# Attention and mixture-of-depths on one core: the gate taken from the gathered rows, a shorter index, and a redrawn order of work

## The chip, the cores and the metric

The kernel runs on one core of a Trainium2 chip. The metric is the device time of one execution in microseconds. The kernel before takes 217.61 us, the median of three runs (217.41 to 217.83).

## The reference

The inputs are q, k and v of 8 batches, 12 heads, 448 tokens and 64 features, a gate vector of 768, and two weight matrices. All arrays are fp32.

```python
scores = scale * np.matmul(q, k.transpose(0, 1, 3, 2))       # scale = 1/8
attn = np.maximum(scores, 0.0) ** 2 / S                      # S = 448
x = np.matmul(attn, v)                                       # heads side by side: [8, 448, 768]
# then, for each batch b
s = x @ w_gate                                               # one score a token
top_idx = the 128 tokens with the highest s
xe = x[top_idx]
ye = np.maximum(xe @ w1, 0.0) @ w2                           # 768 -> 1024 -> 768
out = x;  out[top_idx] = x[top_idx] + sigmoid(s[top_idx])[:, None] * ye
```

## The kernel before

One program does everything, and the order of its work is written out by hand: `ORDER` is a string of some 1,350 items such as `S,6,2,1`. The loop at the end reads them one by one and calls the function of that name, so each engine's queue holds its instructions in the order of the string. Engines run in order, each waits on semaphores where a tile isn't ready, and a waiting instruction holds up all that is behind it on its engine.

**Attention.** A batch has six pairs of heads, numbered t = 6b to 6b + 5, and two pairs make a unit u (u = 0, 2, 4 are batch 0, u = 6, 8, 10 are batch 1, and so on to u = 46). `T,u` transposes q and k of a unit on TensorE (112 small matmuls) into two PSUM banks; `TE,t,engine` copies one pair's result to SBUF on ScalarE (A) or VectorE (D). For the first unit q and k are apart: `Tq`, `Tk`, `TEq`, `TEk`. `S,u,i,banks` makes the scores of 64 keys, i = 0 to 6, in one of two pairs of banks. `R,u,i` (L242) is their relu on ScalarE into SBUF. `Q,u,g` (L249) squares a group of two or three of them on VectorE. `V,u,i` multiplies with v and sums over i in two banks; `X,t,engine` copies the result, transposed x, to SBUF. Only ScalarE does R, only VectorE does Q.

**Experts.** For batch b: `g` (six matmuls with the gate vector repeated over 128 columns) gives the scores as rows, `bc` copies them to SBUF, `col` and `colE` turn them into columns. `XR` and `XRE` transpose x back to rows (for the last batches the DMA transpose `XB` does it, and `XP`, `XPE` for the last two pairs). `rk` counts for each token how many score higher, `less` (six 1-column matmuls) adds the counts across blocks, and `hot` makes a one-hot matrix of the chosen tokens. `xe` gathers the chosen rows with that matrix, already transposed, `xeE` copies them out. `h` and `hE` are the first expert layer (eight blocks in two halves), `y` and `yE` the second, with the gate as the scale of `yE`. `ST` writes the batch's plain rows to the output and `ADD` adds the gated rows with an indirect DMA. The last batch does without the addition: `xs` gathers its chosen rows, `yX` adds them, and `PUT` writes them.

**The gate and the index before.** `tok` holds for each token its number, in two parts, and its score in three bf16 parts, made by the four VectorE operations of `p` (L362, L364, L366, L368). `sel` multiplies the one-hot matrix with these five columns. `sE` then copies the result (L408), adds the two parts of the number into `idx` (L410) and the three parts of the score into `g_` (L412), and `sig` (L416) takes the sigmoid on ScalarE. `tok` has four copies, for batches in flight together.

**Loads.** All but the first q, the gate vector and the DMA transposes are issued by GpSimd (POOL). `L,b,i,r` loads half r (six heads) of q, k or v (i = 0, 1, 2) of batch b and casts it to bf16; `W,0` and `W,1` load w1 and w2. From batch 3 on a load also waits for a given R, so that the loads are spread (`PACE`). `Zp` builds constants on GpSimd and stands among the loads. The gate vector `wgf` is loaded by SyncE inside `C,0`, after a memset on VectorE, and `Zw` spreads it on VectorE.

**Zero matmuls.** `D,n,cols,bank` issues n matmuls of zeros that nobody reads.

A tile in PSUM takes one of eight banks by its tag, and a bank is used again when its last reader is done. The matmuls of all the helpers but `col` have line L179.

## Time and profile before

| | us |
|---|---|
| median of three runs | 217.61 |
| the profiled execution, its time | 217.12 |
| its span, first to last instruction | 215.4 |
| TensorE matmuls busy | 196.4 (91%) |
| ScalarE busy | 181.7 (84%) |
| VectorE busy | 174.8 (81%) |
| GpSimd busy | 71.6 (33%) |
| 168 score evictions R on ScalarE | 144.1 |
| 72 squarings Q on VectorE | 88.8 |

The mean granted clock of TensorE is 0.989. Busy shares are averages over a start, a long stretch in which attention of one batch and experts of another run side by side, and a last stretch that has experts alone; what counts is the engine that the others wait for in each of them. A TensorE that is called busy may be waiting, since the ends of matmuls are modelled.

### The profile page before, as it was taken

The page shows a single profiled execution, that of the slowest core. Times are in us where ns is not written, and L with a number is a line of the kernel's source. Part 1 is how long each engine was busy: PE and PEld are TensorE (multiplying, and loading weights), DVE is VectorE, ACT ScalarE, POOL GpSimd, SP SyncE. Part 2 cuts the span into 40 slices and gives each one's busy share as a digit, 9 for nine tenths or more (in the row PEclk, how much of TensorE's full clock was granted, in tenths as well). Part 3 has the DMA queues.
Part 4 walks back from the last instruction along what each step waited for, and adds up shares of the span by engine and source line. Part 5 has one row for each costly group of instructions (what it writes and reads, how often), then busy time and mean ns, then how long its engine had stood idle before and what let it go on. Part 6 is the DMA issues. An engine that isn't in the chain of part 4 may idle for free. (4 is left out here: it accounts for less than half of the span.)

```text
span 215.4 us, 8419 instructions
## 1 busy us (share of the span) xinstructions
PE 196.4 (91%) x3745; PEld 118.4 (55%) x3745; DVE 174.8 (81%) x355; ACT 181.7 (84%) x252; POOL 71.6 (33%) x103
## 2 busy tenths in 40 slices
...
GB/s 118 171 174 201 207 213 206 206 209 271 270 206 306 237 166 6 251 233 110 130 87 330 177 134 64 148 309 135 65 142 210 83 50 163 148 98 159 137 64 73
DMA packets 32532, 35.90 MB, mean 167 GB/s; under 512 B 7728, under 2 KB 29872, under 8 KB 31600
## 3 DMA queue, kind: packets, MB, share of 16 engines
...
q10 hardware_dynamic: 144, 0.23, 0.4%
q14 instruction: 7, 0.06, 0.1%
...
## 5 line engine op out<-in xcount | busy, mean ns | idle before, releaser
L242 ACT ACTIVATE r_sb<-s_ps 128x896 bf16<-128x896 f32 x168 | 144.1, 940 | 5.1 <-PE s_ps L179 4.9
L249 DVE TENSOR_TENSOR a_sb<-r_sb 128x1792 bf16<-128x1792 bf16 (+1 forms) x72 | 88.8, 1247 | 4.2 <-ACT r_sb L242 3.9
L179 PE MATMUL s_ps<-qkt 64*64 64x448 bf16 x672 | 62.9, 372 | 4.3 <-ACT r_sb L242 2.8
L179 PE MATMUL o_ps<-a_sb,v_sb 64*64 64x448 bf16 x672 | 46.2, 360 | 2.2 <-DVE a_sb L249 2.1
L179 PEld LDWEIGHTS <-qkt 64*64 64x64 bf16 x672 | 24.4, 105 | 29.6 <-issue 17.9
L268 DVE COPY qkt<-t_ps 128x896 bf16<-128x896 bf16 (+1 forms) x38 | 22.1, 604 | 8.8 <-PE t_ps L179 8.8
L179 PE MATMUL ye_ps<-w_sb,hT 128*128 128x384 bf16 x128 | 27.9, 329 | 0.4 <-ACT hT L264 0.4
L179 PEld LDWEIGHTS <-v_sb 64*64 64x64 bf16 x672 | 20.5, 107 | 13.4 <-issue 7.5
L179 PE MATMUL h_ps<-xeT,w_sb 128*128 128x128 bf16 x384 | 27.9, 220 | 0.0
L179 PEld LDWEIGHTS <-w_sb 128*128 128x128 bf16 x384 | 22.1, 98 | 7.8 <-issue 7.2
L82 POOL DMA_DIRECT2D q_sb<-in_q_dram x18 | 11.9, 667 | 39.5 <-ACT r_sb L242 38.2
L270 DVE TENSOR_SCALAR xT_sb<-o_ps 128x448 bf16<-128x448 f32 x28 | 17.1, 621 | 7.1 <-PE o_ps L179 6.9
L82 POOL DMA_DIRECT2D k_sb<-in_k_dram x20 | 14.5, 732 | 21.1 <-ACT r_sb L242 17.4
L82 POOL DMA_DIRECT2D v_sb<-in_v_dram x18 | 11.9, 672 | 27.0 <-ACT r_sb L242 17.9
L489 POOL DMA_INDIRECT out_dram<-gye,idx x7 | 13.8, 1966 | 10.9 <-ACT xeT L264 5.7
L179 PEld LDWEIGHTS <-hT 128*128 128x128 bf16 x128 | 10.6, 97 | 10.9 <-issue 6.3
L374 DVE SCALAR_TENSOR_TENSOR trash<-bc_sb,cols,tie 64x64 bf16<-64x64 f32 (+3 forms) x32 | 14.5, 477 | 0.7
L179 PE MATMUL xe_ps<-hot_sb,x_sb 128*128 128x128 bf16 x192 | 14.4, 219 | 0.1
L179 PE MATMUL sc_ps<-xT_sb,wg_rep 128*128 128x448 bf16 x48 | 13.7, 354 | 0.6 <-DVE xT_sb L270 0.5
L264 ACT ACTIVATE xT_sb<-o_ps 128x448 bf16<-128x448 f32 x20 | 11.3, 572 | 3.4 <-PE o_ps L179 3.4
L264 ACT ACTIVATE qkt<-t_ps 128x896 bf16<-128x896 bf16 (+1 forms) x12 | 10.3, 864 | 4.1 <-PE t_ps L179 4.0
L179 PEld LDWEIGHTS <-x_sb 128*128 128x128 bf16 x192 | 11.3, 97 | 4.2 <-issue 3.4
...
## 6 DMA issues: line engine op xcount, KB each, us to landing
...
```

The source lines that it names most:

```text
L82: return [nc.gpsimd.dma_start(out=t_sb[b % NBUF][HALF[r], h0:h1], in_=heads(src, b, r, h0, h1)) for r in halves]
L179: nc.tensor.matmul(out=out_, lhsT=lhsT, rhs=rhs, start=start, stop=stop, skip_group_check=True, **kw)
L242: relus[u, i] = nc.scalar.activation(out=r_sb[u, g][:, i - GROUP.index(g)], in_=s_ps.pop((u, i))[:, :, :S], func=AF.Relu).ins
L249: nc.vector.tensor_tensor(out=a_sb[u, g], in0=r, in1=r, op=ALU.mult)
L264: nc.scalar.activation(out=out_, in_=in_, func=func or AF.Copy, scale=scale)
L268: nc.vector.tensor_copy(out=out_, in_=in_)
L270: nc.vector.tensor_scalar(out=out_, in0=in_, scalar1=scale, scalar2=None, op0=ALU.mult)
L374: nc.vector.scalar_tensor_tensor(out=self.more[p, c, 128 * c:], in0=self.bc_[p, 128 * c:S], scalar=self.cols[p, c:c + 1], in1=tie[p, :S - ...
L489: nc.gpsimd.indirect_dma_start(out=out[0:self.b + 1].rearrange("b s d -> (b s) d"), out_offset=bass.IndirectOffsetOnAxis(ap=self.idx[:, :1 ...
```

## The change

- **Gate.** For all batches but the last, the score of a chosen row is computed again from the gathered row: ahead of the first `y` of half 0, six 1-column matmuls multiply the gathered rows with one column of the repeated gate vector, into a 385th column of y's bank, and `sig` reads that column from PSUM. `p` is left out for these batches, and `tok` has one copy. The last batch keeps the old way.
- **Index.** `sE,0` adds the two parts of the number straight from PSUM into `idx`. For all but the last batch `sel` has two columns and `sE,0` is the only one of the three operations.
- **Order.** The whole string is redrawn. Among other things: `C,0` is now on VectorE and `C,1` on ScalarE; `TEq` stands ahead of `Tk`; the loads of batches 1 and 2 and of the weights come in another order (q and k of batch 2 ahead of w1), and `Zp` stands among the last of them; `T,6` and `T,10` come ahead of the `V` of unit 4, `T,18` ahead of the scores of unit 16; `XP` of the last two pairs comes behind the last two `g`. Counting the letters, ScalarE has 5 fewer TE, 3 fewer X and 1 fewer yE, and 3 more XRE, 3 more hE and 2 more xeE; VectorE has the reverse.
- **Zero matmuls.** 55 in place of 33: eleven in place of eight of 512 columns at the start, and 44 in place of 25 of 128 columns, the later ones up to the scores of unit 6.

```diff
--- before.py
+++ after.py
@@ -123,8 +123,7 @@
     slot_row = const.tile([128, NC, CAP], mybir.dt.float16)
     tie = const.tile([128, S], BF16)
     chosen = const.tile([CAP, HD], FP32)
-    NTK = 4
-    tok = const.tile([128, NTK, NC, 5], BF16)
+    tok = const.tile([128, NC, 5], BF16)
 
     def Zp():
 
@@ -133,7 +132,7 @@
 
         for r in range(2):
             for i in range(2):
-                nc.gpsimd.iota(tok[HALF[r], :, :, i], pattern=[[0, NTK], [i, NC]], base=4 * i * r,
+                nc.gpsimd.iota(tok[HALF[r], :, i], pattern=[[i, NC]], base=4 * i * r,
                                channel_multiplier=4 - i, allow_small_or_imprecise_dtypes=True)
 
 
@@ -326,13 +325,13 @@
         def __init__(self, b):
             self.b = b
             self.xT = xT_sb[b % NX]
-            self.tk = tok[:, b % NTK]
+            self.last = b == B - 1
             self.bc_ = bc_sb[b % 2]
             self.hot_ = hot_sb[b % 2]
             self.more = trash_[b % 2]
             for pool, name, shape, dt in (
                     (tiny, "cols", [128, NC], FP32), (tiny, "rem", [128, NC], FP32),
-                    (tiny, "rank_", [128, NC], FP32), (tiny, "sel_", [CAP, 5], FP32),
+                    (tiny, "rank_", [128, NC], FP32), (tiny, "sel_", [CAP, 3], FP32),
                     (tiny, "idx", [CAP, 1], INT32), (tiny, "g_", [CAP, 1], FP32)):
                 setattr(self, name, pool.tile(shape, dt, name=name))
             self.ps = {}
@@ -357,7 +356,8 @@
             nc.vector.tensor_copy(out=self.cols, in_=self.ps["col"])
 
         def p(self, i):
-            tk, cols, rem = self.tk, self.cols, self.rem
+
+            tk, cols, rem = tok, self.cols, self.rem
             if i == 0:
                 nc.vector.tensor_copy(out=tk[:, :, 2], in_=cols)
             elif i == 1:
@@ -398,22 +398,25 @@
                                         op1=ALU.is_equal)
 
         def sel(self, at):
-            self.ps["sel"] = bank(at, [CAP, 5], FP32, "sel_ps")
+            n = 5 if self.last else 2
+            self.ps["sel"] = bank(at, [CAP, n], FP32, "sel_ps")
             for c in range(NC):
-                mm(self.ps["sel"], self.hot_[:, c, :], self.tk[:, c, :], c == 0, c == NC - 1)
+                mm(self.ps["sel"], self.hot_[:, c, :], tok[:, c, :n], c == 0, c == NC - 1)
 
         def sE(self, i):
             sel = self.sel_
             if i == 0:
-                nc.vector.tensor_copy(out=sel, in_=self.ps["sel"])
+                nc.vector.tensor_scalar(out=self.idx, in0=self.ps["sel"][:, 0:1],
+                                        scalar1=self.ps["sel"][:, 1:2], scalar2=None, op0=ALU.add)
             elif i == 1:
-                nc.vector.tensor_tensor(out=self.idx, in0=sel[:, 0:1], in1=sel[:, 1:2], op=ALU.add)
+                nc.vector.tensor_copy(out=sel, in_=self.ps["sel"][:, 2:5])
             else:
-                nc.vector.scalar_tensor_tensor(out=self.g_, in0=sel[:, 4:5], scalar=sel[:, 3:4],
-                                               in1=sel[:, 2:3], op0=ALU.add, op1=ALU.add)
+                nc.vector.scalar_tensor_tensor(out=self.g_, in0=sel[:, 2:3], scalar=sel[:, 1:2],
+                                               in1=sel[:, 0:1], op0=ALU.add, op1=ALU.add)
 
         def sig(self):
-            nc.scalar.activation(out=self.g_, in_=self.g_, func=AF.Sigmoid)
+            nc.scalar.activation(out=self.g_, in_=self.g_ if self.last else self.ps["y", 0][:, 384:385],
+                                 func=AF.Sigmoid)
 
         def xe(self, half, mi, at=None):
             if mi == 0:
@@ -460,7 +463,7 @@
 
         def yX(self, half):
             cols = slice(half * 384, half * 384 + 384)
-            nc.vector.scalar_tensor_tensor(out=self.gye[:, cols], in0=self.ps["y", half],
+            nc.vector.scalar_tensor_tensor(out=self.gye[:, cols], in0=self.ps["y", half][:, :384],
                                            scalar=self.g_[:, 0:1], in1=chosen[:, cols],
                                            op0=ALU.mult, op1=ALU.add)
 
@@ -477,12 +480,17 @@
             if f == 0:
                 if not hasattr(self, "gye"):
                     self.gye = gye_pool.tile([CAP, HD], FP32, name="gye")
-                self.ps["y", half] = bank(at, [CAP, 384], FP32, "ye_ps")
-            mm(self.ps["y", half], self.hT[:, f, :], w2_sb[:, f, half * 384:half * 384 + 384],
+                self.ps["y", half] = bank(at, [CAP, 385], FP32, "ye_ps")
+                if half == 0 and not self.last:
+
+                    for m in range(NM):
+                        mm(self.ps["y", half][:, 384:385], self.xeT[:, m, :], wg_rep[:, m, 0:1],
+                           m == 0, m == NM - 1)
+            mm(self.ps["y", half][:, :384], self.hT[:, f, :], w2_sb[:, f, half * 384:half * 384 + 384],
                f == 0, f == NF - 1)
 
         def yE(self, half, eng):
-            put(eng, self.gye[:, half * 384:half * 384 + 384], self.ps["y", half],
+            put(eng, self.gye[:, half * 384:half * 384 + 384], self.ps["y", half][:, :384],
                 scale=self.g_[:, 0:1])
 
         def ADD(self):
@@ -493,106 +501,104 @@
                 compute_op=ALU.add)
 
     ORDER = """
-    D,8,512,4 C,0,A C,1,D Tq,0,7,6 Tk,0 TEq,0,A TEq,1,D TEk,1,D TEk,0,A D,7,128,4 S,0,1,1 S,0,0,0 R,0,1 R,0,0
-    D,6,128,4 S,0,6,1 T,2,7,6 R,0,6 S,0,2,0 TE,2,D Zw,D R,0,2 D,3,128,4 S,0,4,1 L,1,1,0 TE,3,D R,0,4 D,3,128,4
-    S,0,3,0 Q,0,0 L,1,0,1 R,0,3 D,3,128,4 S,0,5,1 L,1,0,0 R,0,5 D,3,128,4 S,2,4,0 L,1,1,1 Q,0,1 V,0,0,7,6 V,0,1
-    V,0,2 Zp S,2,2,1 T,4,5,4 Q,0,2 R,2,2 V,0,3 V,0,4 R,2,4 TE,5,D S,2,0,1 V,0,5 V,0,6 TE,4,D L,1,2,0 R,2,0
-    S,2,1,0 X,1,D L,1,2,1 R,2,1 X,0,D S,2,5,1 W,0 R,2,5 g,0,0,7 Q,2,0 g,0,1 S,2,3,0 L,2,0,1 S,2,6,1 R,2,3
-    L,2,1,0 V,2,0,6,5 R,2,6 Q,2,1 L,2,0,0 V,2,1 V,2,2 S,4,2,0 L,2,1,1 S,4,4,1 R,4,2 Q,2,2 V,2,3 V,2,4 W,1 R,4,4
-    S,4,3,0 V,2,5 L,2,2,1 V,2,6 R,4,3 S,4,1,1 X,2,D L,2,2,0 R,4,1 X,3,D S,4,0,0 g,0,2 Q,4,1 g,0,3 R,4,0 S,4,5,1
-    R,4,5 S,4,6,0 Q,4,0 R,4,6 V,4,0,6,5 Q,4,2 V,4,1 V,4,2 V,4,3 V,4,4 V,4,5 V,4,6 X,4,A X,5,D T,6,6,4 XR,0,0,5
...
-    h,1,0,1 R,16,5 h,1,0,2 Q,16,1 V,16,0,5,4 V,16,1 V,16,2 L,4,2,1 h,1,1,2 Q,16,2 h,1,1,3 V,16,3 hE,1,1,A V,16,4
-    V,16,5 V,16,6 g,2,0,6 X,16,D X,17,A g,2,1 g,2,2 g,2,3 T,18,5,4 g,2,4 TE,18,A TE,19,D h,1,0,3 g,2,5 hE,1,0,D
...
-    V,46,5 V,46,6 h,6,0,0,7 X,46,D X,47,A h,6,0,1 SC,44 XP,47,5 XP,46,6 XPE,47,A g,7,4 g,7,5 XPE,46,D h,6,0,2
-    bc,7,A SC,47 sel,6,6 h,6,0,3 sE,6,0 col,7,5 sE,6,2 sE,6,1 hE,6,0,A colE,7 rk,7,2 SC,46 sig,6 y,6,1,0,7
...
+    D,11,512,4 C,0,D C,1,A Tq,0,7,6 TEq,0,A TEq,1,D D,7,128,4 Tk,0 TEk,0,A TEk,1,D D,5,128,4 S,0,1,1 S,0,0,0
+    R,0,1 R,0,0 D,6,128,4 S,0,2,1 Zw,D T,2,7,6 R,0,2 S,0,5,0 TE,3,D R,0,5 L,1,1,1 D,3,128,4 S,0,3,1 Q,0,0
+    L,1,1,0 R,0,3 D,3,128,4 S,0,4,0 L,1,0,0 R,0,4 TE,2,D D,3,128,4 S,0,6,1 V,0,0,6,5 L,1,0,1 V,0,1 V,0,2 R,0,6
+    Q,0,1 S,2,2,0 L,2,0,0 T,4,7,4 R,2,2 S,2,3,1 L,1,2,0 Q,0,2 V,0,3 V,0,4 R,2,3 L,2,0,1 S,2,1,0 TE,4,D V,0,5
+    L,1,2,1 R,2,1 S,2,0,1 TE,5,D V,0,6 L,2,1,1 R,2,0 X,0,D S,2,5,0 L,2,1,0 X,1,D D,2,128,4 g,0,0,7 R,2,5 S,2,4,1
+    Q,2,0 W,0 g,0,1 R,2,4 S,2,6,0 W,1 R,2,6 D,3,128,4 S,4,0,1 Q,2,1 V,2,0,6,5 V,2,1 L,2,2,1 V,2,2 R,4,0 S,4,3,0
+    Q,2,2 V,2,3 Zp V,2,4 R,4,3 S,4,4,1 D,2,128,4 V,2,5 R,4,4 V,2,6 S,4,1,0 X,2,D R,4,1 L,2,2,0 D,2,128,4 S,4,2,1
+    Q,4,1 g,0,2 R,4,2 D,2,128,4 S,4,5,0 X,3,D R,4,5 D,2,128,4 T,6,6,4 Q,4,0 g,0,3 TE,6,A S,4,6,1 R,4,6 TE,7,D
+    D,4,128,5 T,10,6,5 S,6,0,0 TE,10,D TE,11,A S,6,1,1 Q,4,2 V,4,0,6,4 R,6,1 V,4,1 V,4,2 V,4,3 V,4,4 R,6,0 V,4,5
+    V,4,6 S,6,2,1 X,4,D R,6,2 S,6,4,0 X,5,D T,8,6,5 R,6,4 L,3,0,0 S,6,5,1 Q,6,0 XR,0,2,4 g,0,4 R,6,5 g,0,5
+    S,6,3,0 bc,0,A TE,9,D L,3,0,1 S,6,6,1 R,6,3 TE,8,D XR,0,0,7 XR,0,1,5 XRE,0,2,D R,6,6 XR,0,3,6 Q,6,1 col,0,4
+    S,8,1,0 XRE,0,0,A S,8,5,1 colE,0 Q,6,2 XRE,0,3,A V,6,0,7,4 V,6,1 V,6,2 R,8,1 V,6,3 V,6,4 rk,0,0 V,6,5 V,6,6
+    R,8,5 S,8,0,0 rk,0,1 rk,0,2 R,8,0 L,3,1,1 S,8,2,1 hot,0,0 rk,0,3 less,0,6 R,8,2 X,6,D S,8,3,0 hot,0,1
+    hot,0,2 R,8,3 g,1,0,7 L,3,1,0 hot,0,3 S,8,4,1 XRE,0,1,D sel,0,6 R,8,4 Q,8,0 ST,0 xe,0,1,0,5 xe,0,1,1
+    xe,0,1,2 X,7,A S,10,1,0 S,8,6,1 xeE,0,1,A g,1,1 sE,0,0 Q,8,1 R,8,6 xe,0,0,0,4 xe,0,0,1 xe,0,0,2 R,10,1
+    V,8,0,6,5 Q,8,2 S,10,0,1 V,8,1 V,8,2 V,8,3 R,10,0 S,10,2,0 V,8,4 xeE,0,0,D V,8,5 V,8,6 R,10,2 S,10,3,1 X,8,D
+    h,0,0,0,4 h,0,0,1 X,9,A L,3,2,0 Q,10,0 h,0,0,2 R,10,3 h,0,0,3 S,10,6,0 hE,0,0,A T,12,6,5 R,10,6 S,10,4,1
...
+    xe,1,1,2 T,18,6,5 xeE,1,1,D S,16,1,1 X,13,A Q,14,2 S,14,4,0 sel,1,7 R,14,4 h,1,1,0,4 h,1,1,1 sE,1,0 TE,18,D
...
+    y,1,1,0,7 y,1,1,1 y,1,1,2 y,1,1,3 colE,2 sig,1 y,1,1,4 XRE,2,2,A rk,2,1 S,20,0,0 XR,2,3,4 rk,2,0 R,20,0
+    y,1,0,2 y,1,0,3 y,1,0,4 y,1,0,5 XRE,2,3,D R,20,2 y,1,0,6 y,1,0,7 hot,2,0 S,18,5,0 ST,2 rk,2,3 T,22,6,4
...
+    y,2,0,5 R,24,6 bc,3,D XR,3,1,7 S,26,1,0 XRE,3,1,D sig,2 col,3,6 R,26,1 y,2,1,0,4 y,2,0,6 colE,3 y,2,0,7
+    rk,3,0 S,24,5,1 yE,2,0,A V,24,0,7,6 V,24,1 rk,3,3 S,26,2,0 R,24,5 rk,3,1 XR,3,0,5 y,2,1,1 y,2,1,2 R,26,2
...
+    XRE,4,3,D XR,4,1,6 colE,4 L,7,0,1 hE,3,1,A rk,4,0 y,3,0,0,7 XRE,4,1,A y,3,0,1 rk,4,1 S,30,6,1 T,32,5,4 sig,3
+    R,30,6 hot,4,0 S,30,3,0 rk,4,3 XR,4,2,6 TE,33,D R,30,3 y,3,0,2 y,3,0,3 TE,32,D y,3,0,4 y,3,0,5 y,3,0,6
...
+    y,4,0,0,5 XRE,5,2,D R,36,6 XR,5,3,7 colE,5 rk,5,1 S,36,3,0 sig,4 XRE,5,3,A T,38,6,4 rk,5,0 S,36,5,1 R,36,3
+    y,4,0,1 TE,38,D y,4,0,2 y,4,0,3 y,4,1,0,7 y,4,0,4 TE,39,D R,36,5 y,4,0,5 y,4,0,6 y,4,0,7 Q,36,1 XR,5,0,6
...
+    S,42,5,1 XB,41 Q,42,0 S,44,2,0 bc,6,A y,5,1,0,6 y,5,0,0,5 R,42,5 y,5,0,1 y,5,0,2 col,6,7 sig,5 Q,42,2
+    y,5,0,3 R,44,2 S,44,0,1 y,5,0,4 y,5,0,5 R,44,0 y,5,1,1 colE,6 S,44,3,0 rk,6,0 V,42,0,7,4 V,42,1 R,44,3
...
+    hE,6,0,A V,46,4 V,46,5 V,46,6 h,6,1,0,6 X,46,A X,47,D h,6,1,1 g,7,4 g,7,5 y,6,0,0,5 bc,7,A XP,47,4 sig,6
+    col,7,7 XPE,47,D SC,44 h,6,1,2 colE,7 h,6,1,3 rk,7,0 y,6,1,0,7 y,6,1,1 hE,6,1,A y,6,1,2 y,6,1,3 rk,7,2 SC,47
+    XP,46,4 y,6,1,4 rk,7,1 y,6,1,5 XPE,46,A y,6,1,6 y,6,1,7 y,6,0,1 hot,7,0 less,7,6 p,7,0 yE,6,1,A rk,7,3 SC,46
...
```

155 lines of the change are left out of this document (67 added, 88 removed).

## The prediction

> **What bounds the kernel now.** I read the busy shares of the page, then the table of stretches, cut at the first score eviction R of batch 0 (9.76 us), the first of batch 1 (33.22) and the end of the last one (192.70). Columns after the stretch: its length, busy time (count) of PE, PEld, DVE, ACT, POOL, then clock, DMA share, GB/s.
>
> ```profile
> PE 196.4 (91%) x3745; PEld 118.4 (55%) x3745; DVE 174.8 (81%) x355; ACT 181.7 (84%) x252; POOL 71.6 (33%) x103
> ...
> L242 ACT ACTIVATE r_sb<-s_ps 128x896 bf16<-128x896 f32 x168 | 144.1, 940 | 5.1 <-PE s_ps L179 4.9
> ```
>
> ```profile
> 0.00:9.76 9.76, 6.31 (x79) 2.84 (x79) 2.29 (x15) 3.04 (x5) 8.12 (x18) 1.00 0.85 138
> 9.76:33.22 23.46, 18.49 (x376) 9.78 (x372) 18.47 (x22) 19.36 (x25) 13.23 (x22) 1.00 1.20 199
> 33.22:192.70 159.48, 155.96 (x3115) 94.53 (x3112) 144.85 (x289) 153.56 (x212) 42.56 (x54) 0.99 0.88 171
> 192.70:215.40 22.70, 15.60 (x184) 11.27 (x182) 9.18 (x31) 5.74 (x12) 7.72 (x10) 0.97 0.79 113
> ```
>
> From the first R to the last, ScalarE (ACT) is the thread that everything hangs on: 168 R take 144.1 us, 0.86 each, and no other engine does them. In the long stretch ACT idles 159.48 - 153.56 = 5.92 us, TensorE (PE) 3.52, VectorE (DVE) 14.63. So the time there is ACT's work plus its stalls, with PE close behind. In the head, 9.76 to 33.22, ACT idles 23.46 - 19.36 = 4.10 us. The last 22.70 us are one chain through the last batch's experts.
>
> The sum is made against the profiled execution: span 215.4, time 217.12, so 1.72 us lie around the span. The median of the runs is 217.61, 0.49 above it; I add that at the end.
>
> **The head: first R.** The chain of the start is in ACT's timeline.
>
> ```profile
> 8.09 0.98 ACT L264 ACTIVATE qkt<-t_ps 128x448 bf16<-128x448 bf16 x2 [2.09 <-PE t_ps L179]
> 9.76 0.92 ACT L242 ACTIVATE r_sb<-s_ps 128x896 bf16<-128x896 f32 x1 [0.69 <-PE s_ps L179]
> ```
>
> TEq and TEk run back to back after both transposes, 0.98 us. The new order puts TEq ahead of Tk, so that it fills the wait for k, and only TEk is left behind the transposes: half of 0.98, so **-0.5**. Bounds: 0, if k's landing is late anyhow, and -0.75, if the three more 512-column zero matmuls bring full clock before the first scores. The other added zero matmuls (33 before, 55 now) stand where PE waits for R or a landing; they cost nothing as long as ACT is behind, else each as much as a short PE slice.
>
> C,0 moves to DVE, and with it the gate vector's load: its memset now follows the cast of q.
>
> ```profile
> wgf<-in_moe_w_gate_dram SPq DMA_DIRECT2D x1, 3.0 KB, 5.4
> ```
>
> It was issued early on SP's otherwise empty queue; now it starts near 5.9 us, after the cast. With the same 5.4 to landing it comes at 11.3, and Zw, TE,3 and the first square Q wait behind it on DVE. PE's first V and S,2 wait for those. I leave 0.8 us of ACT idle in the head for this (bounds 0 and 2.5).
>
> **The head: batch 1's first transposes.** ACT's timeline, then PE's, then POOL's issue of loads:
>
> ```profile
> 30.39 0.55 ACT L264 ACTIVATE xT_sb<-o_ps 128x448 bf16<-128x448 f32 x1 [1.79 <-PE o_ps L179]
> 31.71 0.92 ACT L264 ACTIVATE qkt<-t_ps 128x896 bf16<-128x896 bf16 x1 [0.78 <-PE t_ps L179]
> 33.22 0.92 ACT L242 ACTIVATE r_sb<-s_ps 128x896 bf16<-128x896 f32 x1 [0.15 <-PE s_ps L179]
> ```
>
> ```profile
> 28.62 1.73 PE L179 MATMUL o_ps<-a_sb,v_sb 64*64 64x448 bf16 x28 [1.21 <-DVE a_sb L249]
> 30.98 0.41 PE L179 MATMUL t_ps<-ident,q_sb 64*64 64x64 bf16 x28 [0.64 <-ACT xT_sb L264]
> ```
>
> ```profile
> 20.54 0.66 POOL L82 DMA_DIRECT2D q_sb<-in_q_dram  x1 [0.94 <-DMA q_sb<-in_q_dram]
> 22.22 0.66 POOL L82 DMA_DIRECT2D k_sb<-in_k_dram  x1 [1.03 <-DMA q_sb<-in_q_dram]
> 23.93 0.89 POOL L168 DMA_DIRECT2D w_sb<-in_moe_w_dram  x1 [1.05 <-DMA k_sb<-in_k_dram]
> ```
>
> POOL's waits end on landings, one load about every 1.7 us. The last of batch 1's q and k is in by 23.93, yet T,6 stands behind all of V,4 and starts at 30.98, waiting for an eviction and not for data. The new order sets T,6 and T,10 before V,4, after 20 of the 21 R of batch 0. The first four loads of batch 1 stay first (k, k, q, q), so the data is there. Of the head's 4.10 us idle all but the 0.8 goes: **-3.3**. Bounds: 0, if DVE's squares are late (its 18.47 busy us in the head must then fit before TE,7), and -4.1.
>
> What is late next: W1 now queues behind four more loads (q and k of batch 2).
>
> ```profile
> L166 POOL DMA_DIRECT2D w_sb<-in_moe_w_dram x1: 876/876/876, 17.4 to 17.4; - x1
> ...
> DMA to landing us min/median/max: 18.3/18.3/18.3
> ```
>
> It landed at 35.7; four times 1.7 makes 42.5. Its first reader h,0,0 stands behind R,10,2: batch 1's first R near 29, 17 R at 0.86, some four evictions of about 0.6, less one R that PE runs ahead, so near 45. It is hidden with 2.5 us to spare. W2 has the same loads ahead as before.
>
> **ACT against DVE.** Counting the letters in both orders, ACT loses five TE and three X and one yE and gains three XRE, three hE and two xeE.
>
> ```profile
> L264 ACT ACTIVATE xT_sb<-o_ps 128x448 bf16<-128x448 f32 x20 | 11.3, 572 | 3.4 <-PE o_ps L179 3.4
> ...
> L264 ACT ACTIVATE qkt<-t_ps 128x896 bf16<-128x896 bf16 x10 | 9.3, 929 | 2.0 <-PE t_ps L179 1.9
> ...
> L264 ACT ACTIVATE x_sb<-x_ps 128x768 bf16<-128x768 bf16 x7 | 5.7, 820 | 0.1
> ...
> L264 ACT ACTIVATE hT<-h_ps 128x512 bf16<-128x512 f32 x6 | 3.6, 605 | 3.4 <-PE h_ps L179 3.4
> ...
> L264 ACT ACTIVATE xeT<-xe_ps 128x384 bf16<-128x384 f32 x6 | 3.0, 526 | 0.0
> ...
> L264 ACT ACTIVATE gye<-ye_ps,g__514 128x384 f32<-128x384 f32 x2 | 1.2, 616 | 0.0
> ```
>
> 5 x 0.929 + 3 x 0.572 + 0.616 - 3 x 0.820 - 3 x 0.605 - 2 x 0.526 = 1.65; neighbours overlap by about 0.1 (R: 940 ns long, 858 apart), so **-1.5**, on the path. Bounds -1.7 and 0, the latter where PE sets the pace.
>
> DVE drops the three-way split of the scores in seven batches and two of the three operations on sel.
>
> ```profile
> L362 DVE CAST tok<-cols 128x4 bf16<-128x4 f32 x8 | 1.5, 182 | 0.0
> ...
> L366 DVE CAST tok<-rem 128x4 bf16<-128x4 f32 x8 | 1.4, 169 | 0.0
> L368 DVE TENSOR_TENSOR tok<-rem,tok 128x4 bf16<-128x4 f32 x8 | 1.3, 164 | 0.0
> ...
> L364 DVE TENSOR_TENSOR rem<-cols,tok 128x4 f32<-128x4 f32 x8 | 1.3, 158 | 0.0
> ...
> L408 DVE COPY sel__4942<-sel_ps 128x5 f32<-128x5 f32 x1 | 0.2, 166 | 0.8 <-PE sel_ps L179 0.8
> ```
>
> Seven times 0.673 is 4.7 us less, and two small operations in seven batches another 2.3 at 0.166. What DVE takes over from ACT and gives back nearly cancels. I cost all of it at 0: DVE has 14.63 idle us in the stretch. Bounds -1 (squares earlier) and 0.
>
> **The gate from the rows.** Six 1-column matmuls in seven batches, 42 in all, each with a 128x128 weight load, like those of less:
>
> ```profile
> 38.60 0.41 PE L179 MATMUL less_ps<-ones,trash 128*128 128x1 bf16 x6
> ```
>
> 42 x 0.41 / 6 = 2.9 us on PE, an upper end since the 0.41 has a matmul's own latency once. PE has 3.52 idle us in the stretch, so a part shows: **+0.7**, near the lower end because ACT and not PE holds the path; ends 0 and +2.9. [...] The sigmoid now reads y's bank, so the matmuls of y's half 0 that follow it in the order wait for ACT. That is a new wait; its rival is below.
>
> **Stalls of the long stretch.** ACT's timeline:
>
> ```profile
> 77.39 0.60 ACT L264 ACTIVATE hT<-h_ps 128x512 bf16<-128x512 f32 x1 [1.19 <-PE h_ps L179]
> ...
> 79.72 0.92 ACT L264 ACTIVATE qkt<-t_ps 128x896 bf16<-128x896 bf16 x1 [0.87 <-PE t_ps L179]
> ```
>
> ```profile
> 40.63 4.16 ACT L242 ACTIVATE r_sb<-s_ps 128x896 bf16<-128x896 f32 x5 [0.78 <-PE s_ps L179]
> ```
>
> The pair around 78 us (2.06) is the head's fault again: T,18 comes after V,16, with no scores left to evict. The new order has T,18 ahead of S,16,1. I take -1.5, since PE's h, V and g of that place must still be done somewhere. The 0.78 stands in a stretch of half clock:
>
> ```profile
> 39.86:43.27 3.41, 3.26 (x34) 1.57 (x37) 2.96 (x8) 2.64 (x4) 1.24 (x2) 0.50 1.18 211
> 36.44:39.85 3.41, 1.87 (x20) 0.85 (x20) 3.20 (x9) 3.41 (x5) 1.21 (x2) 1.00 1.26 205
> ```
>
> PE was busy 1.87 of 3.41 us before the clock fell. With batch 1 earlier and zero matmuls between, that stretch is fuller: -0.6. Together **-2.1**; ends 0 and -2.8. [...]
>
> **The tail.** XP of pairs 47 and 46 moves behind the last two g:
>
> ```profile
> 195.06 0.62 PE L179 MATMUL x_ps<-ident,xT_sb 128*128 128x128 bf16 x8
> ```
>
> The chain g, bc, col, rk starts up to 0.62 earlier: **-0.5**, ends 0 and -0.6. From xe,7 on PE has the same work.
>
> **Sum.** -0.5 - 3.3 - 1.5 + 0.7 - 2.1 - 0.5 = -7.2: 217.12 - 7.2 = 209.9, and 210.4 against the median.
>
> **The rivals.**
> - PE sets the pace of the long stretch. For it: PE is busy 155.96 of 159.48 us, and the gates add to it. Against it: busy PE holds waits too, and ACT idles only 5.92. Then only start, head and tail gain, and the gates cost 0.7: 217.61 - 0.5 - 3.3 - 0.5 + 0.7 = 214.0. Chance 0.20.
> - Nearly all of ACT's stalls go. For it: DVE is lighter and every T earlier. 217.61 - 0.5 - 4.1 - 1.5 - 5.0 - 0.5 = 206.0. Chance 0.12.
> - Slower: PE waits for the sigmoid. In batches 1 to 6 some of y's half 0 stands behind sig in the order and writes the bank that sig reads; that a wait covers a whole bank is seen in TEq, which at 8.09 waited for Tk. If ACT is two R (1.9 us) behind each time, six batches cost 11.3: 217.61 - 7.2 + 11.3 = 221.7. It decides from 7.2 / 6 = 1.2 us in each batch. Against it: scores placed between sig and y already make PE wait for the R before. Chance 0.06.
> - The redrawn order gives back what it gains in small waits and the time stays at 217.6. Chance 0.02.
>
> My forecast has 0.60: likeliest 210.4, by itself 207.5 to 213. The range 206 to 215 takes in the two other gains. A measurement of this kernel tells about 0.2% from no change; faster by more than that 0.91, within it 0.02, slower 0.07.
>
> **What would show it.** First R near 9.2 and batch 1's first R near 29; no ACT idle over 1 us before T,6 or T,18; full clock near 40 us; ACT busy about 1.5 us less; PE not waiting for ACT's sig; W1's readers not waiting. It is wrong if the long stretch keeps its 159 us, or if a wait for a weight, for wgf or for sig stands where the old ones went.

## The result, and the profile after

The changed kernel takes 214.89 us (median of 20 runs, 211.83 to 218.77) against 217.00 for the kernel before on the same chip: a ratio of 0.987, 95% interval 0.984 to 0.991. The ratio, here and below, is that of the fast runs, without the executions that took over 1.5% more than their kernel's fastest, so it is not quite the ratio of the medians. The kernel is faster, by 1.3% and not by the 3.3% predicted. The profiled execution takes 215.07 us, with a span of 213.3; the profile before is of one execution too.

Two lines of the page of the changed kernel, and its table of stretches, cut at the same events as before (first R, batch 1's first R, end of the last R; the columns are those of the prediction's table):

```profile
PE 193.7 (91%) x3809; PEld 123.6 (58%) x3809; DVE 171.0 (80%) x314; ACT 181.0 (85%) x251; POOL 72.4 (34%) x103
...
L241 ACT ACTIVATE r_sb<-s_ps 128x896 bf16<-128x896 f32 x168 | 144.4, 947 | 9.2 <-PE s_ps L178 8.3
```

```profile
0.00:8.55 8.55, 6.49 (x87) 3.00 (x87) 2.34 (x15) 3.15 (x5) 7.32 (x17) 1.00 0.79 137
8.55:30.85 22.30, 17.62 (x412) 10.89 (x412) 16.79 (x20) 19.13 (x23) 13.98 (x23) 0.92 1.25 193
30.85:190.65 159.80, 153.81 (x3128) 97.89 (x3120) 142.94 (x251) 152.84 (x211) 43.39 (x54) 0.99 0.91 177
190.65:213.30 22.65, 15.76 (x198) 11.85 (x194) 8.96 (x29) 5.89 (x12) 7.74 (x10) 0.91 0.64 98
```

Stretch by stretch against before: start 9.76 to 8.55, head 23.46 to 22.30, long stretch 159.48 to 159.80, tail 22.70 to 22.65. The whole gain lies ahead of batch 1's first R. In the long stretch ScalarE and VectorE have less to do than before, and the time is the same (161.58 in a second profile of the changed kernel, `after_again`); over the whole span ScalarE's waits for scores grew from 4.9 to 8.3 us.

Three timelines of the changed kernel show what is new: VectorE's in the head, then ScalarE's, then TensorE's (start, length, instruction, and in brackets the idle time ahead of it with what ended it).

```profile
12.12 0.56 DVE L267 CAST wg_rep<-wgf 128x768 bf16<-128x768 f32 x1 [4.18 <-DMA wgf<-in_moe_w_gate_dram]
```

```profile
16.43 0.92 ACT L241 ACTIVATE r_sb<-s_ps 128x896 bf16<-128x896 f32 x1 [2.10 <-PE s_ps L178]
...
30.85 2.53 ACT L241 ACTIVATE r_sb<-s_ps 128x896 bf16<-128x896 f32 x3 [0.78 <-PE s_ps L178]
```

```profile
62.09 0.94 PE L178 MATMUL o_ps<-a_sb,v_sb 64*64 64x448 bf16 x16
64.87 0.38 PE L178 MATMUL s_ps<-qkt 64*64 64x448 bf16 x4 [1.84 <-issue]
```

The gate vector landed at 12.1, and the spread `Zw` and the squares behind it held up the first V and so ScalarE. And TensorE stands still for 1.84 us at 63 us for no semaphore at all ("issue" means that the engine waited for nothing that the profile shows). The waits of the long stretch, summed by what ended them, TensorE's of the changed kernel and then of the kernel before (total, number, longest):

```profile
PE s_ps L178 <- issue: 1.8, 1, 1.8
PE s_ps L178 <- ACT r_sb L241: 1.8, 3, 1.0
PE o_ps L178 <- issue: 0.7, 2, 0.5
PE t_ps L178 <- issue: 0.7, 1, 0.7
```

```profile
PE s_ps L179 <- ACT r_sb L242: 1.4, 4, 0.4
PE t_ps L179 <- issue: 0.8, 1, 0.8
PE s_ps L179 <- issue: 0.5, 1, 0.5
```

### The profile page after: what moved, and what is told of

Read it like the earlier page. It is cut to its first block, busy times and chain, and to the rows that moved or that the text cites. A ratio compares the mean times of both kernels' runs of the same rounds, so it can differ in the third digit from the quotient of the medians.

```text
span 213.3 us, 8530 instructions
## 1 busy us (share of the span) xinstructions
PE 193.7 (91%) x3809; PEld 123.6 (58%) x3809; DVE 171.0 (80%) x314; ACT 181.0 (85%) x251; POOL 72.4 (34%) x103
## 5 line engine op out<-in xcount | busy, mean ns | idle before, releaser
L178 PE MATMUL o_ps<-a_sb,v_sb 64*64 64x448 bf16 x672 | 44.7, 360 | 2.4 <-DVE a_sb L248 1.6
L178 PEld LDWEIGHTS <-v_sb 64*64 64x64 bf16 x672 | 21.5, 107 | 13.1 <-issue 5.4
L267 DVE COPY qkt<-t_ps 128x896 bf16<-128x896 bf16 (+1 forms) x43 | 24.7, 605 | 4.0 <-PE t_ps L178 3.9
L178 PE MATMUL h_ps<-xeT,w_sb 128*128 128x128 bf16 x384 | 26.7, 220 | 0.0
L269 DVE TENSOR_SCALAR xT_sb<-o_ps 128x448 bf16<-128x448 f32 x31 | 18.5, 618 | 7.7 <-PE o_ps L178 7.7
L497 POOL DMA_INDIRECT out_dram<-gye,idx x7 | 14.6, 2089 | 14.9 <-DVE gye L269 8.8
L82 POOL DMA_DIRECT2D k_sb<-in_k_dram x20 | 14.4, 733 | 15.1 <-ACT r_sb L241 11.3
L82 POOL DMA_DIRECT2D v_sb<-in_v_dram x18 | 11.9, 670 | 22.5 <-ACT r_sb L241 19.9
L313 POOL DMA_DIRECT2D out_dram<-x_sb x7 | 3.8, 548 | 36.1 <-DMA x_sb<-xT_sb 14.0
L374 DVE SCALAR_TENSOR_TENSOR trash<-bc_sb,cols,tie 128x448 bf16<-128x448 f32 (+3 forms) x32 | 14.1, 477 | 0.6
L178 PEld LDWEIGHTS <-x_sb 128*128 128x128 bf16 x192 | 12.0, 102 | 3.9 <-issue 3.1
L178 PE MATMUL x_ps<-ident,xT_sb 128*128 128x128 bf16 x152 | 12.3, 219 | 0.1
```

The lines of the kernel that those rows point to most:

```text
L82: return [nc.gpsimd.dma_start(out=t_sb[b % NBUF][HALF[r], h0:h1], in_=heads(src, b, r, h0, h1)) for r in halves]
L178: nc.tensor.matmul(out=out_, lhsT=lhsT, rhs=rhs, start=start, stop=stop, skip_group_check=True, **kw)
L267: nc.vector.tensor_copy(out=out_, in_=in_)
L269: nc.vector.tensor_scalar(out=out_, in0=in_, scalar1=scale, scalar2=None, op0=ALU.mult)
L313: nc.gpsimd.dma_start(out=rows[:, 0:4], in_=x_rows[b][HALF[0]])
L374: nc.vector.scalar_tensor_tensor(out=self.more[p, c, 128 * c:], in0=self.bc_[p, 128 * c:S], scalar=self.cols[p, c:c + 1], in1=tie[p, :S - ...
```

## The experiments

Times are medians. The runs were made on four chips, and the kernel before took 217.1 to 218.2 us beside them, so ratios to it are given with their intervals.

**The first four: what the parts cost.** `after_again` is the changed kernel once more. `wgf_first` moves the memset and load of the gate vector:

```diff
+    nc.vector.memset(wgf, 0.0)
+    nc.sync.dma_start(out=wgf, in_=moe_w_gate.rearrange("(m p) -> p m", p=128))
     unit_f = const.tile([1, 1], FP32)
...
-        if hh == 0:
-            nc.vector.memset(wgf, 0.0)
-            nc.sync.dma_start(out=wgf, in_=moe_w_gate.rearrange("(m p) -> p m", p=128))
```

`gate_alone` is the order of before with the new gate (`p,b,*`, `sE,b,1`, `sE,b,2` dropped for b < 7, `sig,b` ahead of the first `yE,b`). `old_gate_new_order` is the reverse:

```diff
-            self.last = b == B - 1
+            self.last = True
+            self.tk = tok[:, b % NTK]
...
-    sE,0,0
+    sE,0,0 sE,0,1 sE,0,2
```

and so in batches 1 to 6, with each of the four `p,b,*` behind one of the four `rk,b,*`.

> The changed kernel once more, as the measure for its neighbours. Two theories of why the long stretch (batch 1's first R to the last R) kept its 159.8 us: A, ScalarE's stream of R still sets the pace and lost its gain to a few single stalls; B, TensorE's stream, in order, sets the pace. Single stalls that belong to the order must come back at the same place in this profile (the 1.78 us wait of ScalarE at 65.30, the half clock from 14.85 and from 66.05 us); stalls that belong to the one execution move. Time as before it: 214 to 215.5, 1.3% under the kernel before.

> The gate vector's memset and load go ahead of everything else on VectorE, as early as in the kernel before; nothing else changes. If the late gate vector holds up the head (VectorE idle 4.18 us before Zw, then ScalarE 2.10 us before the first R behind the squares, and half clock from 14.85 to 18.26 us), the first R of batch 1 comes near 28.8 instead of 30.85 and the whole time falls by about 2 us, to 213. The rival, that the batch's squares or the loads of q and k hold the head anyhow, gives no change: batch 1's first R stays within 0.5 us of 30.85.

> The kernel before with its own order of work, but the gate of batches 0 to 6 computed from the gathered rows, the index by one addition, the three-way split of the scores dropped in those batches, and sig placed just ahead of the first yE of its batch. If ScalarE sets the pace (A), nothing changes by more than 0.5 us: 217 against 217. If TensorE does (B), the 42 more matmuls show: 1 to 2.9 us slower. If VectorE's 7 us of small operations had been in the way of the squares, it is 1 to 3 us faster. If TensorE waits for sig where half 0 of y goes on behind it (batches 3 and 6 in this order), those two waits show as TensorE idle of 1 to 2 us each, released by ScalarE.

> The changed kernel's order, with the gate again carried through the selection: the three-way split of the scores (right behind the four rk), three operations on sel right behind it, no gate matmuls, sig at the same place but reading VectorE's sum. If TensorE sets the pace (B): 1 to 2.9 us faster than the changed kernel. If ScalarE does (A): within 0.5 us. If the new order needs the lighter VectorE: slower by up to the 7 us of small operations, seen as more waits of TensorE for a_sb and hot_sb.

Measured: `after_again` 215.55 us (0.993, 0.990 to 0.996); `wgf_first` 214.04 (0.986, 0.982 to 0.990); `gate_alone` 220.55 (1.018, 1.013 to 1.022); `old_gate_new_order` 214.23 (0.988, 0.984 to 0.992).

In `after_again` TensorE's stall at 63 us (1.81) and half clock from 14.3 and 65.5 us came back, as expected of things that belong to the order. In `wgf_first` ScalarE has no wait in batch 0 any more, and batch 1's first R comes at 28.43, close to the 28.8 of its theory, against 30.61 in `after_again`:

```profile
9.70 15.49 ACT L240 ACTIVATE r_sb<-s_ps 128x896 bf16<-128x896 f32 x19
...
28.43 3.35 ACT L240 ACTIVATE r_sb<-s_ps 128x896 bf16<-128x896 f32 x4 [0.74 <-PE s_ps L177]
```

That is 2.2 us at that point. At the end 1.5 were left (215.55 to 214.04): TensorE's stall at 60 us, the one just seen at 63, had grown from 1.8 to 3.2.

The late gate vector does not cost 2.2 us by itself, though. `load_waits`, further down, is the same as the changed kernel up to 55 us, and there the vector landed at 11.22 instead of 12.12. Below are ScalarE in `load_waits`, and then 14.85 to 18.26 us in the changed kernel and in `load_waits`; the third figure from the end is the granted clock.

```profile
14.83 10.63 ACT L241 ACTIVATE r_sb<-s_ps 128x896 bf16<-128x896 f32 x13 [0.36 <-PE s_ps L178]
...
28.78 4.16 ACT L241 ACTIVATE r_sb<-s_ps 128x896 bf16<-128x896 f32 x5 [0.80 <-PE s_ps L178]
```

```profile
14.85:18.26 3.41, 3.41 (x88) 2.51 (x87) 3.41 (x5) 1.63 (x2) 2.08 (x4) 0.50 1.27 205
```

```profile
14.85:18.26 3.41, 2.99 (x86) 1.35 (x72) 3.41 (x6) 3.41 (x5) 2.44 (x4) 1.00 1.27 205
```

Four profiles with the late vector had half clock there, and batch 1's first R at 29.94 to 30.85; three others with the same start (`act_lighter`, `load_waits`, `old_gate_new_order`) kept full clock and had it at 29.29, 28.78 and 28.47. So most of the 2.2 us goes with half clock; at full clock the late vector costs 0 to 0.9.

By the medians the gate itself costs 3.8 us (1.8%) in `gate_alone`, and taking it out of the new order gains 1.3, more than theory A by ScalarE allowed. These are not yet prices of the gate's work, as the next rounds show: `old_gate_new_order` has the full clock at the start that `after_again` lacks, and 84 instructions of TensorE less.

**Who sets the pace of the long stretch.** Below are the edits of `act_lighter`, `zeros_as_before` and `loads_later`, cut out of the order; items on one line of the first two do not stand side by side in it. Of the zero matmuls left out, `D,2,128,4` stands at five places and the `D,3,128,4` is that behind `R,2,6`. `wgf_first_old_gate` joins `wgf_first` and `old_gate_new_order`.

```diff
-    XRE,0,3,A XRE,2,2,A XRE,4,2,A XRE,5,0,A
+    XRE,0,3,D XRE,2,2,D XRE,4,2,D XRE,5,0,D
```

```diff
-    D,11,512,4
+    D,8,512,4
...
-    D,2,128,4 D,3,128,4 D,4,128,5
```

```diff
-    XRE,1,0,A L,4,0,1 Q,12,2
+    XRE,1,0,A Q,12,2
...
-    yE,0,1,A ST,1 T,16,7,5
+    yE,0,1,A T,16,7,5
...
-    R,14,2 hot,1,3
+    R,14,2 L,4,0,1 ST,1 hot,1,3
```

> The changed kernel with the zero matmuls of the kernel before: 8 instead of 11 wide ones at the start, and without the 17 that stand between batch 0's last scores (five times two, once three, once four). A third theory, C: the idle stretches of TensorE that no engine ends (1.16 us at 28.8 to 29.1, 1.8 us at 63.0, both again in the second profile of the changed kernel, each with a 16 KB packet of instructions landing within or just ahead of it) are TensorE waiting for its own instructions, after a stretch with many short ones. By C, with 17 matmuls and their weight loads (34 instructions) less ahead of it, the gap at 28.8 shrinks below 0.6 us or goes; the one at 63 stays. By the prediction's reading, zero matmuls cost nothing and keep the clock up: the gap stays at 1.1, a stretch of half clock comes back between 20 and 45 us, and the time is 0.5 us longer. The first R moves by less than 0.3 us in both.

> The changed kernel with four of ScalarE's evictions of gathered-order rows (XRE of batches 0, 2, 4, 5, 0.82 us each) given to VectorE: ScalarE's work in the long stretch falls by 3.3 us. If ScalarE sets the pace (A): 2.5 to 3.3 us faster. If TensorE does (B), or its instructions (C): within 0.7 us, and ScalarE's idle time in the long stretch grows from 7 to some 10 us.

> The changed kernel with one load (batch 4's q, second half, issued at 58.7 us) and the store of batch 1's rows (62.2 us) moved behind R,14,2, near 67 us, so that the DMA engines carry less between 59 and 65 us. If TensorE's gap of 1.8 us at 63 is its instructions waiting behind that traffic, it shrinks below 0.9 us and the time falls by about 1 us. If it hangs on the number of instructions alone, the gap stays at 1.6 to 2 us. If the moved load is then late for T,24 or the store holds up the next loads, the time is longer by up to 1 us.

> The changed kernel's order with both of the edits that helped: the gate vector loaded first of all, and the gate again carried through the selection. One gave 1.5 us, the other 1.3; if they lie in different stretches they add: 215.55 - 2.8 = 212.7. If both only move the same wait of TensorE for its instructions, 213.8.

Measured: `zeros_as_before` 214.11 us (0.980, 0.974 to 0.986), `act_lighter` 215.22 (0.988, 0.982 to 0.993), `loads_later` 215.33 (0.986, 0.979 to 0.992), `wgf_first_old_gate` 213.43 (0.979, 0.974 to 0.984).

ScalarE's long stretch in `act_lighter`, to set against the third row of the table above:

```profile
29.29:190.23 160.94, 154.08 (x3128) 97.37 (x3120) 144.53 (x255) 151.01 (x207) 45.22 (x54) 0.99 0.91 177
```

Four evictions fewer, ScalarE idle 9.9 us instead of 7.0, and the long stretch of 160.94 us lies between the changed kernel's 159.80 and 161.58, where theory A wanted 2.5 to 3.3 less: ScalarE does not set the pace (theory A falls). `loads_later` told nothing: the load waited for the same R as before, so only its place in POOL's queue had changed. `zeros_as_before` was a miss for both: the stall of 1.16 us at 29 did not shrink, it was 1.21 and ended at 31.74. The half clock between 20 and 45 us did not come back either, so in this one execution the late zero matmuls guarded nothing there.

**Where the stalls stand.** The table of stretches also counts. Here it is cut from the start to just ahead of the instruction that ends a stall, for five stalls of the changed kernel and both stalls of the kernel before; the counts behind the first two busy times are matmuls and weight loads. (One `T` is 56 matmuls and 56 weight loads, so 112 instructions and not 112 matmuls.)

```profile
0.00:30.22 30.22, 23.50 (x479) 13.42 (x480) 18.59 (x35) 22.28 (x28) 21.30 (x39) 0.94 1.12 177
0.00:64.86 64.86, 54.67 (x1119) 33.73 (x1120) 48.50 (x90) 54.51 (x72) 28.79 (x51) 0.97 1.16 204
0.00:103.07 103.07, 91.83 (x1887) 57.44 (x1887) 82.38 (x146) 90.28 (x120) 41.31 (x66) 0.97 1.10 201
0.00:123.52 123.52, 111.56 (x2271) 69.54 (x2271) 101.09 (x179) 110.08 (x148) 47.64 (x73) 0.97 1.05 194
0.00:136.36 136.36, 123.72 (x2527) 77.53 (x2527) 111.97 (x202) 121.92 (x165) 51.39 (x79) 0.97 1.04 192
```

```profile
0.00:40.00 40.00, 29.75 (x607) 15.69 (x608) 26.81 (x55) 29.03 (x37) 22.60 (x42) 1.00 1.13 185
0.00:120.14 120.14, 108.30 (x2143) 63.59 (x2144) 99.03 (x198) 105.09 (x142) 46.09 (x72) 0.99 1.04 196
```

Added up, that is 959, 2239, 3774, 4542 and 5054 and, before, 1215 and 4287. From 959 the others are 5, 11, 14 and 16 times 256 away and, before, 1 and 13 times, to within one. (The expectations below count 193 or 194 above a multiple of 256 where these sums give 190 or 191; what matters is the distance.) TensorE's instructions come in packets of 16 KB, which the page of the changed kernel counts among the DMA queues (packets, MB, share):

```profile
q8 instruction: 30, 0.49, 0.9%
```

That is one packet for every 254 of its 7,618 matmuls and weight loads, close to the 256 of the counts. The packet ahead of the stall at 63 us moved from 62.51 to 63.40, its start 3.9 us after TensorE had entered the block ahead of it (58.60), and TensorE went on at 64.87; the other four stalls above and both of the kernel before ended 1.3 to 1.6 us after such a packet had landed. So I read them as TensorE standing still when it has used up one packet and the next is late. Added up over these boundaries (at each the longest step from one start to the next, if over 0.3 us) the stalls are 1.9 us in the kernel before and 7.1 in the changed one, 1.4 of them ahead of batch 1's first R.

Four runs shift the boundaries and leave the work alone. Small zero matmuls take the place of wide ones at the start, where TensorE waits for q. The diff is that of a shift by 96; for 192 it is `D,1,512,4 Dt,106,4`, and for 160 in the kernel before `D,3,512,4 Dt,85,4` in place of `D,8,512,4`.

```diff
+    def Dt(n, at):
+        ps = bank(at, [128, 512], FP32, "zero_ps")
+        for i in range(n):
+            mm(ps[0:64, 0:64], zero[:, :64], zero[:, :64], True, True)
...
-    D,11,512,4
+    D,7,512,4 Dt,52,4
```

> The changed kernel; of the 11 wide zero matmuls at the start four go and 52 small ones (64 columns) come, in the time in which TensorE waits for q anyway, so that every later instruction of TensorE stands 96 places further on; the work and its order stay. Theory C, now sharper: in all profiles so far TensorE's unexplained idle stretches stand every time where its count of matmuls and weight loads is 193 or 194 above a multiple of 256, the size of a 16 KB packet of instructions of 64 bytes, and they end 1.3 to 1.7 us after that packet landed. Added up they are 1.9 us in the kernel before and 7.1 in the changed one. By C the stall ahead of S,14,1 at 63 us (1.8 to 3.2 us in four profiles) leaves that matmul and stalls stand at other work, again at 193 above a multiple of 256; from the time that the 192 instructions ahead of each new boundary take, I estimate the stalls some 3 us (1 to 5) shorter than without the shift: 212.5. By the rival, that these matmuls wait for something of their own that the profile does not name, the stall stays ahead of the same S and the time stays at 215.

> The same shift by 96 instructions, in the kernel with the gate vector loaded first. By C about 3 us (1 to 5) under that kernel's 214.0: 211, and the 3.2 us stall ahead of S,14,1 gone. By the rival no change: 214.

> The same with a shift by 192 instructions (one wide zero matmul and 106 small ones at the start). By C the stalls move again, to other matmuls; by the same estimate their sum is about that without a shift, so 213 to 215, and slower than the shift by 96. By the rival no change against either.

> The kernel before with a shift by 160 instructions (three wide zero matmuls instead of eight, and 85 small ones, at the start). By C the kernel before had its boundaries at favourable places, 1.9 us of stalls in all; shifted, the estimate is 3 to 4 us more: 220 to 221, with stalls of over 1 us that end 1.3 to 1.7 us after a packet landed. By the rival, 217 as before.

Measured: `shift96_after` 220.99 us (1.019, 1.014 to 1.024), `shift96_wgf_first` 222.38 (1.021, 1.016 to 1.027), `shift192_wgf_first` 214.60 (0.988, 0.982 to 0.993), `shift160_before` 222.19 (1.026, 1.021 to 1.031). The counts at the longest stalls, of `shift96_after` and then of `shift160_before`:

```profile
0.00:32.83 32.83, 26.95 (x607) 15.88 (x608) 21.95 (x38) 25.41 (x32) 20.90 (x40) 1.00 1.13 179
0.00:124.06 124.06, 108.88 (x2271) 68.00 (x2271) 97.95 (x175) 106.40 (x144) 46.58 (x73) 0.99 1.04 193
```

```profile
0.00:104.14 104.14, 91.34 (x1887) 55.77 (x1888) 81.01 (x160) 87.23 (x117) 38.50 (x63) 0.95 1.05 194
0.00:169.89 169.89, 155.66 (x3167) 95.91 (x3168) 141.72 (x282) 150.54 (x204) 56.53 (x86) 0.97 0.97 180
```

1215, 4542, 3775, 6335: the same grid, now at other work; the stall ahead of S,14,1 is gone in `shift96_after` and one of 3.8 us stands in a V at 120. The cause is shown: the same work in the same order takes 5 us more or less by where every 256th instruction falls. Stalls grew by 4.9 us in `shift96_after` (7.1 to 11.9) and the median by 5.4; by 5.0 and 5.0 in `shift160_before`. My estimate of which shift is good was wrong in sign for 96 and right for 160 and 192.

The sum of the stalls is not the whole price. Against `wgf_first` it grew by 2.7 us in `shift192_wgf_first` (7.35 to 10.0) and by 5.5 in `shift96_wgf_first` (to 12.9), and the medians by 0.6 and 8.3. The other part is half clock, which in most profiles begins within about 1.2 us of the end of a long stall (in the changed kernel 1.18 after it, at 66.05). From first to last R, `wgf_first`, `shift192_wgf_first` and `shift96_wgf_first` have clocks of 0.99, 1.00 and 0.97, that is 3.4, 0 and 10.2 us of half clock:

```profile
8.88:190.37 181.49, 170.48 (x3532) 107.65 (x3528) 159.54 (x270) 171.68 (x234) 56.34 (x77) 0.99 0.95 179
```

```profile
9.17:190.59 181.42, 169.41 (x3532) 107.13 (x3528) 160.11 (x270) 171.32 (x234) 56.12 (x76) 1.00 0.95 179
```

```profile
9.65:198.49 188.84, 173.51 (x3532) 109.03 (x3528) 160.06 (x270) 171.49 (x234) 54.87 (x76) 0.97 0.92 171
```

As an estimate, a least-squares fit to the 16 profiles with the new order (those below included) puts the time from first to last R at 173.5 us plus 0.8 us for each us of stall and 0.5 for each us of half clock, with a standard deviation of 0.8 left; with either term alone 1.7 is left.

**What makes a packet late, and what the matmuls cost.** `load_waits` adds to `loads_later` that this load waits for R,14,2. The two `shift128` kernels have `D,6,512,4 Dt,69,4` at the start. `gate_matmuls_unused` is the kernel before with the six gate matmuls into a wider y bank, and nothing reads them. The diffs of the first and the last:

```diff
-            n = PACE[2 * i + r]
+            n = 9 if (b, i, r) == (4, 0, 1) else PACE[2 * i + r]
```

```diff
-                self.ps["y", half] = bank(at, [CAP, 384], FP32, "ye_ps")
+                self.ps["y", half] = bank(at, [CAP, 385], FP32, "ye_ps")
+                if half == 0 and self.b < B - 1:
+                    for m in range(NM):
+                        mm(self.ps["y", half][:, 384:385], self.xeT[:, m, :], wg_rep[:, m, 0:1],
+                           m == 0, m == NM - 1)
```

> The changed kernel, where the second half of batch 4's q now waits for R,14,2 instead of R,12,5, and the store of batch 1's rows stands behind it on POOL's queue: neither moves data between 58 and 66 us. (In loads_later only the order of the issues had changed; the load waited for the same R as before and was issued at the same time.) If the instruction packet waits behind the loads, the one that started 3.4 to 5 us after TensorE entered the block ahead (58.60 to 62.51 in the changed kernel) starts within 2.5 us, and the stall at 63 us of 1.8 to 3.2 us falls below 0.8; time 1 to 1.5 us less: 213.5 to 214.5. If the packet's delay has nothing to do with the loads, the stall stays above 1.6.

> The kernel with the gate vector first, its TensorE instructions shifted by 128 at the start (six wide and 69 small zero matmuls). From 14 profiles: a packet starts some 3 us after TensorE enters the block of 256 ahead while loads run, moves for 0.95 us, and TensorE goes on 1.3 to 1.6 us after it landed; so a block that runs in less than about 5.4 us ends in a stall. Set against the profile's block lengths that gives stalls of 4.9 us for a shift by 128, against 7.0 without one and, for before, 2.6 without one and 10.4 shifted by 160. If that rule foretells, 212 and stalls under 6 us; if the places of the loads matter more than the block's length, anything from 210 to 222.

> The same shift by 128 in the kernel with both helpful edits (gate vector first, gate carried through the selection), which took 213.43 without it. By the rule of block lengths stalls of 4.5 us against 8.6: 209.5 to 211. If the rule is no guide: 213 to 219.

> The kernel before, with the six 1-column gate matmuls of batches 0 to 6 added and their result left unused: the gate still comes through the selection. That is the price of 42 matmuls alone, at the same places in TensorE's stream as in gate_alone (which took 220.55). If the matmuls and the shifted block boundaries are the price, 219 to 221; if sig's new place is (ScalarE waiting for y, TensorE for sig), 217 to 218.

Measured: `load_waits` 215.73 us (0.983, 0.975 to 0.991), `shift128_wgf_first` 218.76 (1.000, 0.993 to 1.006), `shift128_wgf_old_gate` 220.19 (1.012, 1.005 to 1.019), `gate_matmuls_unused` 219.72 (1.010, 1.006 to 1.015).

The load did move, to 67.3, and the stall stayed, 3.5 us: that load was not the cause. Both `shift128` kernels were foretold badly, with stalls of 8.7 and 9.2 us instead of 4.9 and 4.5; the block's length alone is no guide. With the 42 unread matmuls the kernel before takes 1.0% (2.3 us) more. The matmuls themselves hold TensorE for less. In `gate_matmuls_unused`:

```profile
60.95 0.29 PE L179 MATMUL ye_ps<-wg_rep,xeT 128*128 128x1 bf16 x6
61.11 0.32 PE L179 MATMUL ye_ps<-w_sb,hT 128*128 128x384 bf16 x1
```

Six take 0.16 us from start to start (in the changed kernel the starts within a group lie 25 to 39 ns apart), and all 42 take 1.1 us, in `gate_alone` and in the changed kernel as well. What the other 1.2 us are is not shown: stalls hardly grew in that profile (1.9 to 2.1 us), but it is of the fastest execution, only 0.3 us above the profile before. Why `gate_alone` costs 1.5 us more than that is open too, since the two intervals nearly meet; in sig's new place one wait of ScalarE for y shows:

```profile
ACT g__4343 L418 <- PE ye_ps L178: 2.0, 1, 2.0
```

What `load_waits` left moving from 57 to 62 us, beside loads in packets of 896 bytes, was the store of batch 0's rows, issued at 49.7. Over all profiles the packet starts 0.5 us (median) after TensorE enters the block ahead when no data moves, 2.7 beside loads, and all eight stalls over 3 us, with delays of 4.7 to 6.3, stand beside such a store. (A store is counted beside a packet where at least 25 packets of over 4 KB were moving in the 1.2 us ahead of it.) But a store alone does not make a packet late: 86 packets stand beside one, with a median delay of 2.5 us. Two runs move that store:

```diff
-    Q,8,0 ST,0 xe,0,1,0,5
+    Q,8,0 xe,0,1,0,5
...
-    ST,1 T,16,7,5
+    ST,1 ST,0 T,16,7,5
```

> The kernel with the gate vector first, where the store of batch 0's rows is issued right behind that of batch 1 (62 us) instead of near 49, so that its 9 and 12 KB packets no longer move between 57 and 62 us, ahead of the instruction packet for the boundary at 60. If such packets make it late, that packet starts within 3.2 us of TensorE entering the block (4.98 without the edit), and the stall of 3.5 us falls to 1 to 1.8, what the block's 4.07 us leave at the delay of the loads; time 1.5 to 2 us less, about 212.5. If the store has no part, the stall stays at 3.2 to 3.6.

> The same in the kernel with both helpful edits (213.43 without it), where a stall of 1.8 us stood at 63 and one of 2.1, beside the store, at 70 us. If the store is the cause, the second falls by about 1 us and the first does not grow: 212 to 212.8. If not, 213.4.

Measured: `store_later_wgf_first` 213.17 us (0.977, 0.969 to 0.985), `store_later_wgf_old_gate` 212.61 (0.975, 0.968 to 0.982). TensorE at that boundary, in `wgf_first` and then in `store_later_wgf_first`:

```profile
59.40 0.94 PE L177 MATMUL o_ps<-a_sb,v_sb 64*64 64x448 bf16 x16
63.52 0.38 PE L177 MATMUL s_ps<-qkt 64*64 64x448 bf16 x4 [3.19 <-issue]
```

```profile
62.12 0.94 PE L177 MATMUL o_ps<-a_sb,v_sb 64*64 64x448 bf16 x16
63.23 0.38 PE L177 MATMUL s_ps<-qkt 64*64 64x448 bf16 x4 [0.17 <-issue]
```

The delay of the packet fell from 5.0 to 2.1 us and the stall from start to start from 3.5 to 0.5, further than foretold. In the second kernel the stall beside the store kept its 2.1 us, now beside both stores at 66 us, and the other was 1.25. The sums of the stalls did not fall (7.35 to 7.42 and 7.8 to 8.1), others having grown, and the ratios overlap those without the edit. So a store ahead of a packet made one stall, in a single pair of profiles; that moving it shortens the whole is not shown. The three best kernels (0.975, 0.977, 0.979) all lie below the changed one's 0.987; the best, with the gate vector first, the old gate and the later store, has its whole interval below the changed kernel's.

## Why the prediction was wrong

**Right**: the direction; the mechanism of the start (first R at 8.55 instead of 9.2, and seven 128-column zero matmuls ahead of it take 0.56 us instead of 0.93: matmuls became twice as fast near 4.6 us, where the wide zero matmuls go from 0.43 to 0.22 us from start to start, against near 12.4 us in the kernel before, at a granted clock of 1.00 in both; -1.2 against -0.5, beyond my bound of -0.75); the loads (w1's last packet starts at 40.8, so it landed near the 42.5 worked out, and no reader waited for a weight); no matmul of the new order waiting for sig; the stalls at T,6 and T,18. ScalarE's waits other than for scores are nearly gone from the long stretch:

```profile
ACT r_sb L241 <- PE s_ps L178: 5.5, 10, 1.8
ACT xeT L263 <- PE xe_ps L178: 0.9, 1, 0.9
ACT hT L263 <- PE h_ps L178: 0.3, 1, 0.3
```

**Head, -3.3**: the mechanism was right and the size off. First R to batch 1's first R shrank by 1.2; with the vector first it is 28.43 - 8.88 = 19.55, 3.9 less than before, though a stall for instructions of 1.3 us has come into it. I kept 0.8 us for the gate vector, estimated to land at 11.3; it landed at 12.1, TensorE fell to half clock behind the wait (0.50 from 14.85 to 18.26), and together they cost 2.2. Where the clock stayed full it cost 0 to 0.9, within reach of my 0.8. Half clock in the head stood in no term.

**ACT to DVE, -1.5**: not on the path. ScalarE's busy time in the long stretch fell by 0.7 us (153.56 to 152.84), and taking 3.3 us of evictions more off it gained nothing. I read the close busy sums (ScalarE 153.56, TensorE 155.96 of 159.48) as ScalarE leading; it was TensorE's stream.

**Gate, +0.7**: the reason for the lower end was wrong, since ScalarE does not hold the path. The matmuls hold TensorE for 1.1 us, inside 0 to 2.9; with them unread the kernel before takes 2.3 us more, and with the old gate the new order 1.3 less, and neither is a price free of the grid and the clock.

**Stalls of the long stretch, -2.1**: this step failed. The stalls that I named went, and others took their place: TensorE's for its own instructions, 1.9 us before and 7.1 after (1.9 and 5.7 within the long stretch), on which no term and no bound stood. The half clock at 40 us went too, and one from 66.05 came in its place, behind the longest of these stalls. The long stretch was to lose 2.9 us and gained 0.3, which was one of my own signs of being wrong. With two such stalls in the profile of before, both marked "issue", the sum could have carried a term of either sign. The rival in which TensorE sets the pace (214.0) came nearest to the time, but by another mechanism than the one it gave.

**Tail, -0.5**: 0.05 came (22.70 to 22.65). Counted from the last R's end, `bc` starts 0.4 us earlier than before and the first `xe` of the last batch 0.15; the rest was lost on the way between them.

The four stretches add up: -1.21 - 1.16 + 0.32 - 0.05 = -2.10, the span's 215.4 to 213.3. What is missing to -7.2 is 5.1, and the stalls grew by 5.2; that these agree is partly chance, since the start gained and the gate, the half clock and the tail lost beside it.

Still open: what else delays a packet beside loads (half of these packets start 1.4 to 3.5 us after TensorE enters the block ahead), why most stores do not, and how to foretell a good shift.
